# Two attentions on one core: PV ahead of projections when P buffers are full, ScalarE on a unit's last key blocks, VectorE's banks filled when free, gate masks made early

## The chip, the cores and the metric

The kernel runs on one core of a Trainium2 chip. The metric is the device time of one execution in microseconds (us). Three executions of the kernel before took 1019.16, 1023.16 and 1024.05 us; the median, 1023.16 us, is its time.

## The reference

Two attention layers over 2048 positions of width 512, each with 32 heads of 16 columns; their outputs stand side by side.

```python
def _B_ref(x, wqkv, wo):                      # plain softmax attention
    qkv = (x @ wqkv).reshape(B, S, 3, H, Dh) ...
    scores = einsum('bhqd,bhkd->bhqk', q, k) * Dh ** (-0.5)
    o = einsum('bhqk,bhkd->bhqd', softmax(scores), v)
    return merge(o) @ wo

def _A_ref(x, wq, wk, wv, wo, beta):          # 4 segments of 512, with a memory
    g = sigmoid(beta)
    for s in range(4):
        a_dot = softmax(qs @ ks.T * scale + causal_mask) @ vs
        a_mem = (phi(qs) @ M) / (phi(qs) @ z + 1e-6)
        outs.append(g * a_mem + (1 - g) * a_dot)
        M = M + phi(ks).T @ vs;  z = z + sum(phi(ks))
    return merge(outs) @ wo
return concatenate([a, b], axis=-1)
```

## The kernel before

**Units.** The work is cut into 64 units, each four heads over 512 queries: 32 of A (4 segments, 8 head groups) and 32 of B (4 query blocks, 8 head groups). The list `U` sets their order: the 8 units of A's first segment, then B's with A's other units mixed in. The four heads of a unit lie in the four 32-row groups of TensorE, so that four score matmuls, or four PV matmuls in the four column groups, run beside each other.

**Scores and P.** A unit of B has 64 blocks of 128 keys by 512 queries (16 key blocks, 4 heads), each one PSUM bank of scores. Two engines make P from them. ScalarE's blocks (`al`, 45 to a unit) go three and two at a time into two PSUM tiles `s_ps` (L722) and through one exp each (L727) into P tiles `pT`; there are three buffers (`PTB`) for either size, and `pt_out` counts those that PV hasn't read yet. VectorE's blocks (`dl`, 19 to a unit) go singly into one of two banks `d_ps` (L768); VectorE evicts a bank as an integer that is read as f16 (L779), and makes two further copies with an added constant, for two banks at a time (L745); the three together, each with its own scaled V (`VD`, made on POOL at L605), approximate the exp. Tiles `pD` have three buffers (`PDB`). A unit of A has 12 pieces of scores, the exps of L667 and L670, and a triangular mask on POOL (L681).

**PV.** There is one accumulator bank `acc`. PV matmuls (L870, `flush`) are issued for the unit in front alone (`pvi`). When all of its blocks are through, `finalize` transposes the accumulator on VectorE (L808), takes the reciprocal of the row sums (L811) and scales on POOL; only then the next unit's PV begins. ScalarE may be up to three units ahead.

**Projections and other small jobs** are called chores: transposes of x, the projections of q, k and v, the memory of A, the output projections (`chore_q`, `chore_k`, `chore_v`, `chore_out` and so on). Each fills a `d_ps` bank on TensorE, in turn with VectorE's score banks, and is evicted by VectorE. The masks of the queries (L329) are made on POOL behind it.

**What sets the order.** No hardware queue is scheduled by hand. A planner in Python, the loop `while True` in `fast_path`, keeps a model time for TensorE (`c["t"]`), ScalarE, VectorE and POOL, with costs such as 75 + 1.09 n ns for VectorE and 100 + 0.833 n ns for ScalarE, and at each step chooses what to issue next; the order of issue is then that of every engine's queue. A step asks, in this order: a score tile for ScalarE if its PSUM tile is free and fewer than `PTB` P tiles of the size are out (`act_now`), with VectorE banks beside it; a chore or a VectorE bank, if the next `d_ps` bank is free by plan (`dwhen`); PV. A chore has a due time, and it is due at once if `stalled` holds, that is if ScalarE has a unit but neither can take a tile now nor soon. ScalarE's unit `au` is the first of three that still has blocks; a unit of B whose `al` is empty and that has fewer than four blocks of `dl` left is passed over, if its `VD` exists, and VectorE takes the rest.

**The start.** `setup_late` is a chore due at A's third unit: ones in V's extra columns (L132, L133), the masks of the gates `maskg` (L153 to L161), zeros for the memory tiles (L163), and the loads of both `wo` from POOL's queue (L164, L165). The gates themselves come from ScalarE and VectorE at L899 to L902.

## Time and profile before

| | |
|---|---|
| median of three runs | 1023.16 us |
| profiled execution | 1026.3 us |
| its span | 1024.5 us |
| ScalarE (ACT) busy | 855.9 us, 84% |
| TensorE (PE) busy | 812.7 us, 79% |
| VectorE (DVE) busy | 782.7 us, 76% |
| GpSimd (POOL) busy | 375.0 us, 37% |
| mean granted TensorE clock | 0.912 |

The span runs from the first to the last instruction of the profiled execution; the device time has 1.8 us around it. The five compute engines have queues of their own, and each works through its instructions in order; idle time before an instruction is shown with what ended it (`<-engine tile line`). Matmuls overlap, so a busy TensorE is not one at its peak. L numbers are lines of the kernel before; behind line 94 the changed kernel's lines stand 2 to 8 further down (L722 becomes L729, L768 L775, L779 L786, L745 L752, L870 L877, L808 L815).

### The profile page before, as it was taken

The numbers are of one execution on the slowest core, as the hardware profiler recorded it, in microseconds if no ns is written. First come the engines' busy times: TensorE is split into PE (matmuls) and PEld (weight loads), VectorE is DVE, ScalarE is ACT, GpSimd is POOL, SyncE is SP. The second block draws the span as 40 slices with busy tenths as digits, with TensorE's granted clock in tenths as the row PEclk, the third lists the DMA queues.
The fourth block names the chain that finished last, engine by engine and source line by source line (L and its number), as shares of the span: only waits on it lengthen the run. The fifth ranks groups of instructions, "written<-read, shape, count | busy, mean of one in ns | idle before, by whom it ended". The sixth has DMA issues, their size and how long they took to land.

```text
span 1024.5 us, 18143 instructions
## 1 busy us (share of the span) xinstructions
PE 812.7 (79%) x7004; PEld 250.3 (24%) x7004; DVE 782.7 (76%) x1532; ACT 855.9 (84%) x790; POOL 375.0 (37%) x785
## 2 busy tenths in 40 slices
PE   6699888788878777888877777888887788777873
PEld 2233222222222223222222222223222212222221
DVE  3354778888888888778888888796778768889785
ACT  3489998989989598898988899897489689999791
POOL 2860634352144544142432143443542214223320
PEclk9799999998999898998999999899799969989697
DMA  5211000000000000000000000000000000000001
GB/s 169 63 43 36 6 22 2 1 2 1 1 1 17 6 1 12 27 1 2 1 1 22 1 1 2 1 1 22 1 1 2 22 1 2 1 1 1 1 6 40
DMA packets 13951, 13.83 MB, mean 13 GB/s; under 512 B 2336, under 2 KB 13600, under 8 KB 13856
## 3 DMA queue, kind: packets, MB, share of 16 engines
q1 hardware_dynamic: 11808, 10.49, 3.2%
q8 instruction: 56, 0.92, 0.4%
q10 hardware_dynamic: 1632, 1.05, 0.3%
q0 software_dynamic: 416, 1.05, 0.3%
q14 instruction: 39, 0.32, 0.1%
HBM read 8.39 MB, written 4.19 MB: 12 GB/s over the span
## 4 chain that ended last, share of the span: by engine, by line
PE 35%; ACT 34%; issue 17%; DVE 7%; POOL 5%; DMA 1%; ACTq 0%; DVEq 0%
ACT pT L727 30%; PE acc L870 13%; PE s_ps L722 7%; PE d_ps L316 4%; ACT pT L670 4%; PE d_ps L319 3%; DVE pD L779 2%; DVE pD L745 2%; PE s_ps L660 2%; PE d_ps L486 2%; PE d_ps L768 1%; POOL pT L681 1%; POOL VD L605 1%; DMA wk_a<-in_A_wk_dram 1%; DVE tT L808 1%
## 5 line engine op out<-in xcount | busy, mean ns | idle before, releaser
L727 ACT ACTIVATE pT<-s_ps 128x1536 bf16<-128x1536 f32 (+1 forms) x600 | 690.3, 1265 | 93.5 <-PE d_ps L768 55.8
L779 DVE TENSOR_SCALAR pD<-d_ps 128x512 int16<-128x512 f32 x554 | 370.5, 682 | 103.1 <-PE d_ps L768 95.2
L722 PE MATMUL s_ps<-QT_b,KT_b 32*128 32x512 bf16 x1494 | 242.8, 410 | 129.1 <-ACT pT L727 121.5
L870 PE MATMUL acc<-pT,VP_b 128*32 128x512 bf16 x1494 | 274.0, 424 | 1.7 <-DVE tT L808 1.7
L870 PE MATMUL acc<-pD,VD 128*32 128x512 f16 x1662 | 267.3, 425 | 3.6 <-DVE tT L808 2.1
L745 DVE TENSOR_SCALAR pD<-pD 128x1024 int16<-128x1024 int16 x554 | 241.3, 477 | 0.1
L681 POOL TENSOR_SCALAR_AFFINE_SELECT pT<-pT 128x512 bf16<-128x512 bf16 (+3 forms) x192 | 97.1, 518 | 377.5 <-ACT pT L670 361.1
L768 PE MATMUL d_ps<-QT_b,KT_b 32*128 32x512 bf16 x554 | 215.7, 413 | 3.2 <-DVE pD L779 2.1
L670 ACT ACTIVATE pT<-s_ps 128x1280 bf16<-128x1280 f32 (+1 forms) x128 | 138.4, 1191 | 26.0 <-PE s_ps L660 10.8
L722 PEld LDWEIGHTS <-KT_b 32*128 32x128 bf16 x1494 | 70.4, 92 | 348.2 <-issue 344.9
L870 PEld LDWEIGHTS <-VP_b 128*32 128x32 bf16 x1494 | 66.2, 99 | 75.0 <-issue 57.1
L870 PEld LDWEIGHTS <-VD 128*32 128x32 bf16 x1662 | 61.4, 99 | 85.9 <-issue 74.3
L660 PE MATMUL s_ps<-QT_a,KT_a 32*128 32x256 bf16 (+3 forms) x512 | 59.4, 318 | 28.5 <-ACT pT L727 13.0
L605 POOL TENSOR_SCALAR VD<-VP_b 128x288 bf16<-128x288 bf16 (+1 forms) x186 | 66.8, 359 | 12.3
L870 PE MATMUL acc<-pT,VP_a 128*32 128x256 bf16 (+3 forms) x512 | 36.9, 317 | 19.6 <-POOL pT L681 11.3
L829 POOL TENSOR_TENSOR tN<-tT,RA 128x256 bf16<-128x256 f32 x31 | 20.5, 662 | 83.7 <-DVE RA L811 83.6
L768 PEld LDWEIGHTS <-KT_b 32*128 32x128 bf16 x554 | 46.3, 92 | 17.5 <-issue 17.5
L808 DVE STREAM_TRANSPOSE tT<-acc 128x512 f32<-128x512 f32 x64 | 45.1, 704 | 6.0 <-PE acc L870 5.7
L329 POOL TENSOR_SCALAR QT_a<-qc,mq 128x512 bf16<-128x512 bf16 x30 | 21.8, 738 | 54.2 <-DVE qc L385 54.1
L660 PEld LDWEIGHTS <-KT_a 32*128 32x128 bf16 x512 | 20.0, 93 | 86.1 <-issue 78.8
L496 DVE CAST osb<-d_ps 128x512 bf16<-128x512 f32 x28 | 19.4, 691 | 21.8 <-PE d_ps L486 21.7
L329 POOL TENSOR_SCALAR QT_b<-qc,mq 128x512 bf16<-128x512 bf16 x32 | 22.5, 716 | 29.9 <-DVE qc L387 29.6
(110 smaller groups left out, 609.8 us busy)
## 6 DMA issues: line engine op xcount, KB each, us to landing
out_dram<-osb SPq DMA_DIRECT2D x30, 128.0 KB, 1.7
xin<-in_B_x_dram SPq DMA_DIRECT2D x16, 128.0 KB, 2.2
xin<-in_A_x_dram SPq DMA_DIRECT2D x14, 128.0 KB, 2.3
wv_a<-in_A_wv_dram SPq DMA_DIRECT2D x1, 512.0 KB, 10.5
wv_b<-in_B_wqkv_dram SPq DMA_DIRECT2D x1, 512.0 KB, 10.9
wk_b<-in_B_wqkv_dram SPq DMA_DIRECT2D x1, 512.0 KB, 10.8
wq_b<-in_B_wqkv_dram SPq DMA_DIRECT2D x1, 512.0 KB, 10.4
wo_a<-in_A_wo_dram POOLq DMA_DIRECT2D x1, 512.0 KB, 4.8
```

Source lines behind the costliest of these rows:

```text
L329: nc.gpsimd.tensor_scalar(t[:, par, :], qc[:], mq[:, par:par + 1], 1.0, ALU.mult, ALU.mult)
L605: mul = lambda dst, src: nc.gpsimd.tensor_scalar(dst, src, EXP_C[k], 1.0, ALU.mult, ALU.mult)
L660: nc.tensor.matmul(pt[:, b, col:col + w], kt[32 * j:32 * j + 32, kbl * P:(kbl + 1) * P], q[32 * j:32 * j + 32, P * kbl:512], start=(r == 0 ...
L670: nc.scalar.activation(pT[:].rearrange("p b n -> p (b n)")[:, 0:n], pt[:].rearrange("p b n -> p (b n)")[:, 0:n], ACT.Exp, scale=0.25)
L681: nc.gpsimd.affine_select(out=blk, in_=blk, compare_op=ALU.is_ge, fill=0.0, base=0, pattern=[[0, e - b], [0, w // P], [1, P]], channel_mul ...
L722: nc.tensor.matmul(pt[:, b, :], KT_b[32 * j:32 * j + 32, u["rt"], kb * P:(kb + 1) * P], q[32 * j:32 * j + 32, :], start=True, stop=True, t ...
L727: nc.scalar.activation(pT[:, 0:n, :], pt[:, 0:n, :], ACT.Exp, scale=1.0 / (LOG2E * 1024.0))
L745: nc.vector.tensor_scalar(tile[:, k, 0:n, :], tile[:, 0, 0:n, :], EXP_D[k], None, ALU.add)
L768: nc.tensor.matmul(bank[:], KT_b[32 * j:32 * j + 32, u["rt"], kb * P:(kb + 1) * P], qslice(u)[32 * j:32 * j + 32, :], start=True, stop=Tru ...
L779: nc.vector.tensor_scalar(pd[:, 0, n, :], bank[:], EXP_B, 0.0, ALU.add, ALU.max)
L808: nc.vector.transpose(tT[:].rearrange("p c d -> p (c d)"), u["acc"][:])
L870: nc.tensor.matmul(u["acc"][32 * j:32 * j + 32, e["c0"]:512], e["lhsT"], e["rhs"], start=(j not in u["started"]), stop=False, tile_positio ...
```

## The change

```diff
+    nc.sync.dma_start(out=wo_a[:], in_=wview(A_wo))
+    nc.sync.dma_start(out=wo_b[:], in_=wview(B_wo))
...
-    def setup_late():
+    jm = const.tile([P, 4], F32, name="jm")
+    nc.vector.memset(jm[:], 0.0)
+    for j in range(4):
+        nc.vector.memset(jm[32 * j:32 * j + 32, j:j + 1], 1.0)
+    mqg = const.tile([P, 4, 2], F32, name="mqg")
+    def setup_gates():
+        nc.scalar.activation(gcol[:], beta_t[:], ACT.Exp, scale=-1.0)
+        nc.vector.tensor_scalar(gcol[:], gcol[:], 1.0, None, ALU.add)
+        nc.vector.reciprocal(gcol[:], gcol[:])
+        nc.vector.tensor_scalar(omg[:], gcol[:], -1.0, 1.0, ALU.mult, ALU.add)
+        g4, m4 = gcol[:].rearrange("p (r t) -> p r t", t=2), mq[:].unsqueeze(1).to_broadcast([P, 4, 2])
+        nc.vector.tensor_tensor(mqg[:], g4, m4, op=ALU.mult)
+        for par in range(2):
+            to = maskg[:].rearrange("p (r t) j d -> p t r j d", t=2)[:, par]
...
+            for rt in range(4):
+                nc.gpsimd.tensor_tensor(to[:, rt, :, 0:DH], jm[:].unsqueeze(2).to_broadcast([P, 4, DH]),
+                                        mqg[:, rt, par:par + 1].unsqueeze(2).to_broadcast([P, 4, DH]), op=ALU.mult)
         init_v(VP_b, NSB)
...
-        nc.gpsimd.dma_start(out=wo_a[:], in_=wview(A_wo))
-        nc.gpsimd.dma_start(out=wo_b[:], in_=wview(B_wo))
...
-    chore(begin("a", 0, 2), setup_late)
...
+    setup_gates()
...
-            if u["k"] == "b" and nbanks(u) == 0 and len(u["dl"]) < 4 and u["i"] in VD_t:
+            if u["k"] == "b" and exhausted(u):
                 continue
...
-        if ai[0] == len(U) and tail["banks"] is None and ("b", 3, 2) in OT_t and not chores:
+        if ai[0] == len(U) and tail["banks"] is None and ("b", 3, 2) in OT_t:
             tail_open()
...
-        stalled = au is not None and (au["ready"] is None or (act_now is None and act_soon is None))
+        blocked = au is not None and au["ready"] is not None and pt_out[scount[0] % 2][0] >= PTB
+        stalled = au is not None and not blocked and act_now is None and act_soon is None
...
-        dwhen = max(d_when(), c["dve"] - 700)
+        dwhen = d_when()
...
-            while (beside and du["dl"] and max(d_when(), c["dve"] - 700) <= t + 300
+            while (beside and du["dl"] and d_when() <= t + 300
...
+        u = U[pvi[0]]
+        byj = by_head(u, t)
+        rd = sum(byj, [])
+        done = exhausted(u) and len(rd) == len(u["pvq"])
+        full = blocked or max(x[0] for x in pt_out) >= PTB or (dve_out[0] >= PDB and pd_open["tile"] is None)
+        even = min(len(x) for x in byj)
+        if (rd and (even >= 3 or done or (full and len(rd) >= 4) or (blocked and max(len(x) for x in byj) > 0))
+                and (u["acc"] is not None or acc_free[0] <= t + 100) and (act_soon is None or act_soon > t + 200)):
+            flush(u, 16 if done else min(even, 4) if even >= 3 else 3)
+            continue
         if due or du is not None or ch is not None:
...
-        full = max(x[0] for x in pt_out) >= PTB or (dve_out[0] >= PDB and pd_open["tile"] is None)
-        even = min(len(x) for x in byj)
-        if rd and (even >= 3 or done or (full and len(rd) >= 4)) and (u["acc"] is not None or acc_free[0] <= t + 100):
-            if act_soon is None or act_soon > t + 200:
-                flush(u, 16 if done else min(even, 4) if even >= 3 else 3)
-                continue
...
-    assert not chores and tail["banks"] is not None
+    assert tail["banks"] is not None
+    while chores:
+        chores.pop(0)["fn"]()
```

`setup_gates()` is called behind the first transposes of x. The PV step moves ahead of chores and VectorE's banks and is also taken when ScalarE is `blocked` (its unit is ready and its P buffers are full); `blocked` no longer counts as `stalled`. A unit of B stays ScalarE's until all of its blocks are taken. A `d_ps` bank is filled when it is free by plan, without the limit on VectorE's queue. The setup of the gates stands at the start, the loads of `wo` in SP's queue behind the other weights, and chores left over at the end follow the last unit.

Counted over the whole program, VectorE gets 534 score banks for 554 and ScalarE 1514 for 1494, in 303 exps of 1024 columns and 11 of 512, for 296 and 5; those of 1536 remain 299.

On TensorE, in the middle of the program where A's fourth segment begins, a projection of A's queries (`wq_a`), its last two matmuls, and what follows. The kernel before:

```order
9981 L316 LDWEIGHTS wq_a
9982 L316 MATMUL d_ps<-xT_a,wq_a 128x512
9983 L316 LDWEIGHTS wq_a
9984 L316 MATMUL d_ps<-xT_a,wq_a 128x512
9985 L319 LDWEIGHTS xT_a
9986 L319 MATMUL d_ps<-wv_a,xT_a 128x512
```

The changed kernel at the same projection:

```order
10109 L324 LDWEIGHTS wq_a
10110 L324 MATMUL d_ps<-xT_a,wq_a 128x512
10111 L324 LDWEIGHTS wq_a
10112 L324 MATMUL d_ps<-xT_a,wq_a 128x512
10113 L729 LDWEIGHTS KT_b
10114 L729 MATMUL s_ps<-QT_b,KT_b 128x512
```

Before, the next projection follows (here that of V, `wv_a`), and so on for 56 projection matmuls between two score refills; now a score refill for ScalarE (`s_ps`) stands behind the one projection, and one ahead of it.

On VectorE, at the end of the unit that is 51st in the list, a unit of B with one of A behind it. The kernel before (`qc` is the eviction of a projection of queries, `pD<-d_ps` that of score banks, `tT` the transposed accumulator at a unit's end):

```order
797 L387 TENSOR_SCALAR qc<-d_ps 128x512
798 L779 TENSOR_SCALAR pD<-d_ps 128x512 x2
799 L745 TENSOR_SCALAR pD<-pD 128x1024 x2
800 L779 TENSOR_SCALAR pD<-d_ps 128x512 x2
801 L745 TENSOR_SCALAR pD<-pD 128x1024 x2
802 L808 STREAM_TRANSPOSE tT<-acc 128x512
803 L811 RECIPROCAL RA<-tT 128x16
804 L779 TENSOR_SCALAR pD<-d_ps 128x512
805 L808 STREAM_TRANSPOSE tT<-acc 128x512
```

The changed kernel at the end of its 51st unit (`osb` is the eviction of an output projection, `aT` of A's memory):

```order
761 L786 TENSOR_SCALAR pD<-d_ps 128x512 x2
762 L752 TENSOR_SCALAR pD<-pD 128x1024 x2
763 L504 CAST osb<-d_ps 128x512
764 L786 TENSOR_SCALAR pD<-d_ps 128x512
765 L815 STREAM_TRANSPOSE tT<-acc 128x512
766 L818 RECIPROCAL RA<-tT 128x16
767 L474 STREAM_TRANSPOSE aT<-d_ps 128x512
```

Before, four of VectorE's banks are the last work ahead of the transposition, and the next unit's transposition follows at once behind one bank; now two banks, an output projection and one bank stand there, and the next unit's transposition comes later.

On POOL, at the start. The kernel before, from the end of the setup to the masks of the next queries (`mbd` are the memory's tiles):

```order
46 L161 COPY maskg<-bdm 128x4
47 L163 MEMSET mbd_128 128x1024
48 L163 MEMSET mbd_129 128x1024
49 L164 DMA wo_a<-in_A_wo_dram 128x4x512
50 L165 DMA wo_b<-in_B_wo_dram 128x4x512
51 L329 TENSOR_SCALAR QT_a<-qc,mq 128x512 x2
52 L681 AFFINE_SELECT pT_422<-pT_422 128x2x256
```

The changed kernel (the ISA row is the choice of POOL's library):

```order
8 L146 DMA beta_t<-in_A_beta_dram 32x4x2 x4
9 L167 ISA
10 L167 TENSOR_TENSOR maskg<-jm,mq 128x4x4
11 L169 TENSOR_TENSOR maskg<-jm,mqg 128x4x16 x4
12 L167 TENSOR_TENSOR maskg<-jm,mq 128x4x4
13 L169 TENSOR_TENSOR maskg<-jm,mqg 128x4x16 x4
14 L134 MEMSET VP_b 128x32x2 x16
15 L135 MEMSET VP_b 128x16x14
16 L173 MEMSET mbd_130 128x1024
17 L173 MEMSET mbd_131 128x1024
18 L688 AFFINE_SELECT pT_246<-pT_246 128x3x128
```

The setup has moved from behind A's first selects and masks to ahead of the first of them, with fewer operations on the masks and without the two DMAs.

## Rows read from the trace of the kernel before

**Rows 1.** The page: busy us, share of the span and instructions of each engine.

```profile
PE 812.7 (79%) x7004; PEld 250.3 (24%) x7004; DVE 782.7 (76%) x1532; ACT 855.9 (84%) x790; POOL 375.0 (37%) x785
```

**Rows 2.** Busy time by stretch: length, each engine's busy us, granted clock, DMA.

```profile
60.00:1001.00 941.00, 764.82 (x6681) 232.65 (x6680) 750.11 (x1457) 825.21 (x758) 338.48 (x678) 0.92 0.02 7
708.00:732.00 24.00, 20.55 (x115) 7.80 (x113) 18.23 (x31) 5.31 (x6) 14.19 (x23) 0.90 0.05 16
594.00:634.00 40.00, 30.68 (x298) 9.66 (x297) 34.87 (x69) 37.13 (x36) 20.63 (x40) 0.96 0.00 1
```

**Rows 3.** ScalarE in order of time: start, us, what; idle before and what ended it.

```profile
167.70 5.54 ACT L727 ACTIVATE pT<-s_ps 128x1024 bf16<-128x1024 f32 x5 [2.87 <-PE d_ps L768]
...
336.59 0.63 ACT L417 ACTIVATE ek<-kb 128x512 bf16<-128x512 bf16 x1 [4.29 <-DVE kb L410]
343.72 2.37 ACT L727 ACTIVATE pT<-s_ps 128x1536 bf16<-128x1536 f32 x2 [5.58 <-PE d_ps L768]
...
715.27 0.63 ACT L371 ACTIVATE eq<-qc 128x512 bf16<-128x512 bf16 x1 [4.61 <-DVE qc L385]
719.75 0.63 ACT L371 ACTIVATE eq<-qc 128x512 bf16<-128x512 bf16 x1 [3.85 <-DVE qc L385]
727.10 1.02 ACT L727 ACTIVATE pT<-s_ps 128x1024 bf16<-128x1024 f32 x1 [6.72 <-PE s_ps L722]
731.34 7.04 ACT L727 ACTIVATE pT<-s_ps 128x1536 bf16<-128x1536 f32 x6 [3.22 <-PE d_ps L768]
...
818.92 3.83 ACT L727 ACTIVATE pT<-s_ps 128x1536 bf16<-128x1536 f32 x3 [7.40 <-PE s_ps L722]
...
960.76 1.02 ACT L727 ACTIVATE pT<-s_ps 128x1024 bf16<-128x1024 f32 x1 [2.38 <-PE d_ps L768]
```

**Rows 4.** TensorE in order of time, in the second and third episode.

```profile
713.36 1.02 PE L316 MATMUL d_ps<-xT_a,wq_a 128*128 128x512 bf16 x4
...
813.25 0.37 PE L768 MATMUL d_ps<-QT_b,KT_b 32*128 32x512 bf16 x1 [0.67 <-DVE pD L779]
...
817.01 1.26 PE L870 MATMUL acc<-pT,VP_a 128*32 128x512 bf16 x16 [1.52 <-DVE tT L808]
```

**Rows 5.** Groups by line and shape: count, busy us, mean ns, idle before.

```profile
L727 ACT ACTIVATE pT<-s_ps 128x1536 bf16<-128x1536 f32 x299 | 443.0, 1482 | 57.8 <-PE d_ps L768 36.6 <-PE s_ps L722 18.8 <-POOL tN L829 0.7
L779 DVE TENSOR_SCALAR pD<-d_ps 128x512 int16<-128x512 f32 x554 | 370.5, 682 | 103.1 <-PE d_ps L768 95.2 <-PE s_ps L722 3.0
L727 ACT ACTIVATE pT<-s_ps 128x1024 bf16<-128x1024 f32 x296 | 312.7, 1056 | 35.7 <-PE d_ps L768 19.2 <-PE s_ps L722 15.9
L722 PE MATMUL s_ps<-QT_b,KT_b 32*128 32x512 bf16 x1494 | 242.8, 410 | 129.1 <-ACT pT L727 121.5 <-ACT pT L670 5.0
L745 DVE TENSOR_SCALAR pD<-pD 128x1024 int16<-128x1024 int16 x554 | 241.3, 477 | 0.1
L768 PE MATMUL d_ps<-QT_b,KT_b 32*128 32x512 bf16 x554 | 215.7, 413 | 3.2 <-DVE pD L779 2.1 <-DVE qc L387 0.5 <-DVE kb L410 0.5
L727 ACT ACTIVATE pT<-s_ps 128x512 bf16<-128x512 f32 x5 | 3.1, 639 | 0.0
```

**Rows 6.** The start: POOL's mask operation by line, then engines in order of time.

```profile
L159 POOL TENSOR_TENSOR maskg<-bdm,gcol 128x64 f32<-128x64 f32 x8 | 2.3, 294 | 0.1
...
15.26 0.21 ACT L899 ACTIVATE gcol<-beta_t 128x8 f32<-128x8 bf16 x1
...
19.56 1.85 POOL L681 TENSOR_SCALAR_AFFINE_SELECT pT<-pT 128x384 bf16<-128x384 bf16 x4 [15.52 <-issue]
...
32.12 1.46 POOL L132 MEMSET VP_b<- 128x64 bf16 x16
...
38.58 1.84 POOL L163 MEMSET mbd<- 128x1024 bf16 x2
...
42.11 1.37 POOL L329 TENSOR_SCALAR QT_a<-qc,mq 128x512 bf16<-128x512 bf16 x2
...
46.33 2.15 ACT L670 ACTIVATE pT<-s_ps 128x1280 bf16<-128x1280 f32 x2 [10.56 <-POOL QT_a L329]
```

More of the change, by code (lines that the diff above doesn't have):

```diff
@@ L146, in fast_path @@
     gcol = const.tile([P, HG], F32, name="gcol")
-    def setup_late():
-        init_v(VP_b, NSB)
-        bdm = const.tile([P, 2, 4, 17], F32, name="bdm")
-        nc.gpsimd.memset(bdm[:], 0.0)
-        for j in range(4):
-            for par in range(2):
-                nc.gpsimd.tensor_copy(bdm[32 * j:32 * j + 32, par, j, :],
-                                      mq[32 * j:32 * j + 32, par:par + 1].to_broadcast([32, 17]))
-        for hg in range(HG):
-            nc.gpsimd.tensor_tensor(maskg[:, hg, :, 0:DH], bdm[:, hg % 2, :, 0:DH],
-                                    gcol[:, hg:hg + 1].unsqueeze(2).to_broadcast([P, 4, DH]), op=ALU.mult)
-            nc.gpsimd.tensor_copy(maskg[:, hg, :, DH:DH + 1], bdm[:, hg % 2, :, DH:DH + 1])
+    jm = const.tile([P, 4], F32, name="jm")
[12 more added lines that the diff above has]
+            to = maskg[:].rearrange("p (r t) j d -> p t r j d", t=2)[:, par]
+            j4 = jm[:].unsqueeze(1)
+            nc.gpsimd.tensor_tensor(to[:, :, :, DH], j4.to_broadcast([P, 4, 4]), mq[:, par:par + 1].unsqueeze(2).to_broadcast([P, 4, 4]), op=ALU.mult)
+            for rt in range(4):
+                nc.gpsimd.tensor_tensor(to[:, rt, :, 0:DH], jm[:].unsqueeze(2).to_broadcast([P, 4, DH]),
+                                        mqg[:, rt, par:par + 1].unsqueeze(2).to_broadcast([P, 4, DH]), op=ALU.mult)
+        init_v(VP_b, NSB)
         for m in mbds:
             nc.gpsimd.memset(m[:], 0.0)
-        nc.gpsimd.dma_start(out=wo_a[:], in_=wview(A_wo))
-        nc.gpsimd.dma_start(out=wo_b[:], in_=wview(B_wo))
     sat = const.tile([P, 1], F32, name="sat")
@@ L898, in fast_path @@
     nc.vector.tensor_scalar(qt0[:, 1, :], pt[:, 1, :], mq[:, 1:2], None, ALU.mult)
-    nc.scalar.activation(gcol[:], beta_t[:], ACT.Exp, scale=-1.0)
-    nc.vector.tensor_scalar(gcol[:], gcol[:], 1.0, None, ALU.add)
-    nc.vector.reciprocal(gcol[:], gcol[:])
-    nc.vector.tensor_scalar(omg[:], gcol[:], -1.0, 1.0, ALU.mult, ALU.add)
     t0 = c["t"]
@@ L1042, in fast_path @@
             continue
-        u = U[pvi[0]]
-        byj = by_head(u, t)
-        rd = sum(byj, [])
-        done = exhausted(u) and len(rd) == len(u["pvq"])
-        full = max(x[0] for x in pt_out) >= PTB or (dve_out[0] >= PDB and pd_open["tile"] is None)
-        even = min(len(x) for x in byj)
-        if rd and (even >= 3 or done or (full and len(rd) >= 4)) and (u["acc"] is not None or acc_free[0] <= t + 100):
-            if act_soon is None or act_soon > t + 200:
-                flush(u, 16 if done else min(even, 4) if even >= 3 else 3)
-                continue
         if u["acc"] is None:
```

## The prediction

> **What bounds the kernel now.** I read the busy times first [rows 1]: ScalarE has the largest share, 84% of the span, with TensorE at 79% and VectorE at 76%, so no engine is full over the whole run and the ends of its waits decide. Then the busy times by stretch [rows 2]. From 60 to 1001 us ScalarE works 825.2 of 941 us, so it is idle for 115.8 us; the best stretch of 40 us has it busy for 37.1 (93%), and the stretch from 708 to 732 us for only 5.3 of 24 while TensorE there is busy for 20.6. Then the rows of ScalarE with the idle time ahead of each [rows 3]. There are three episodes. From 332 to 344 us it waits 4.29 and 5.58 us, from 710 to 731 us it waits 4.61, 3.85, 6.72 and 3.22 us, and at 811 us it waits 7.40 us: 35.7 us together. Ten more waits of 1.94 to 3.33 us, of which the first (2.87 us at 168 us) and the last (2.38 us at 961 us) stand there, sum to 25.7 us. So 61.4 of the 115.8 us of idle time lie in 17 waits, and the rest in short ones.
>
> The three episodes have two causes, both of the planner. In the second, TensorE runs one projection after another (1.0 us each, [rows 4]) and no score tile: all P buffers are full, the planner calls that "stalled", "stalled" makes any projection due, and projections are asked ahead of PV. Only PV frees a P buffer, so ScalarE stands until the list of projections is empty. In the third, TensorE waits for VectorE's banks (0.67 us at 813 us) and then 1.52 us for the transposition of the accumulator before 16 PV matmuls of the next unit in a row [rows 4]: ScalarE had gone on to later units while the unit in front still had banks for VectorE, and with one accumulator nothing of the later units could be drained.
>
> **The change part by part.** *PV ahead of projections, and "blocked" no longer "stalled".* In the program of before, 10 stretches of TensorE between two score refills hold two or more projections (8 matmuls or more), the longest 56 matmuls; in the changed one a single such stretch is left, of 16. All projections are still there, now mostly one between two refills. At 1.0 us each beside a refill of 0.4 us [rows 5] this makes 1.4 us of TensorE per exp, against exps of 1.48 and 1.06 us [rows 5], mean 1.27: I allow 0.15 us of remaining wait for each of the 24 projections of the three longest stretches, 4 us. *ScalarE takes a unit's last key blocks.* It removes the cause of the third episode and of those among the ten where TensorE drains 16 PV at once. Of the ten I leave 5 us. The gain of these two edits is 61.4 - 4 - 5 = 52 us. Its bounds are 25 us (only the first two episodes go, with 28.3 us, less their projections) and 61.
>
> What the second costs: the program's rows give VectorE 534 banks for 554, and ScalarE 20 more, as seven more exps of 1024 columns and six more of 512. At 1.056 and 0.639 us [rows 5] this is 7.4 + 3.8 = 11.2 us on the engine that sets the path, plus 11.2. VectorE is relieved of 20 evictions (0.682 us) and 20 additions (0.477 us for each bank) [rows 5], 23 us, and TensorE of 40 PV matmuls. Neither ends last over a long stretch, so I count zero; their cover is ScalarE's queue, and if ScalarE were to fall behind them these 23 us would be gain.
>
> ScalarE's share [rows 1] is the largest, and the edit adds to it. The Trainium skill's page Perfetto Trace Analysis, section Identifying the Most-Contended Engine, takes the engine with the highest occupancy as the one to relieve first. A rule that speaks against this edit: by it the 11.2 us would simply lengthen the run, to 1034; the trace bears it out only where ScalarE has no idle time, and 115.8 us of it stand in the middle stretch.
>
> *Banks filled as soon as free.* The limit "VectorE's queue within 700 ns of its end" goes. VectorE loses part of its 103 us of idle time ahead of L779 [rows 5], which isn't on the path: zero. But TensorE's queue is in order, and a bank filled by plan before VectorE has really emptied it holds back the score refills queued behind it, and so ScalarE. In before TensorE waited for this 2.1 us in all [rows 5]. The plan counts an eviction as 633 ns and the trace shows 682; for the two additions of a pair it counts 2 x 403 against 2 x 477, so a pair of banks takes 2.32 us where the plan has 2.07, 0.25 us late. With 267 pairs the cost lies between 0 and 66 us. I take 4, near the row of 2.1, because VectorE has idle time in which to catch up and because ScalarE's exps run longer than planned too (1.48 for 1.38 us), which holds TensorE back first. Some 15 further refills have a projection in front that had none, at 0.15 us 2 us. Together plus 6.
>
> *Gate masks early.* In before POOL goes through the setup from 32.12 to 42.11 us without a pause, with the masks of the next queries behind it, and ScalarE waits 10.56 us for these [rows 6]. This goes. In its place the setup stands ahead of POOL's first select: 8 masks of 0.294 us, the ones of V for 1.46 us, the zeros for 1.84 us, and three small operations that I price like a mask, 0.9 us: 6.5 us together. If it starts as soon as the gates are there, at about 15.5 us, it ends at 22.0, and the first select (19.56 us in before) is 2.4 us late; if POOL can't start before 19.56 us, 6.5 us late. ScalarE has buffers for six tiles before it needs PV, so part is hidden. I take 4: minus 6. ScalarE now computes the gates ahead of the first cast of K, and VectorE four small operations ahead of the first queries. The gates' exp started at 15.26 us behind the cast, without a recorded wait for its data [rows 6], so the cost is 0 to 1.4 us; I take 0.5. The loads of wo pass from POOL to SP, ahead of B's x tiles; these are first needed behind the setup's stall, so zero. The sum of this part is -5.5, with bounds -10 and +1.4.
>
> Of POOL's first operation the profile shows only that 15.52 us went by ahead of it, ended by nothing recorded [rows 6]. The Trainium skill's page GPSIMD Engine Reference, section 2.1 Instruction dispatch, says that the first call after a change of POOL's library costs about 6 us more without a visible instruction. By that the setup would start late, the start would gain nothing, and the time would be 5 us above the forecast; the rows can't tell it apart.
>
> *The end.* Two output projections may now be left for after the last unit: two evictions at the price of L779, 1.4 us [rows 5]. Against that the last unit no longer waits for banks that VectorE still holds. Zero, with 3 us either way.
>
> The sum is -52 + 11.2 + 6 - 5.5 + 0 = -40.3 us. The profiled execution took 1026.3 us, its span of 1024.5 and 1.8 around it; the median of the three runs is 1023.16, and the difference is applied to that: **983 us**. A second way agrees: were the middle stretch as full everywhere as in its best 40 us, it would take (825.2 + 11.2) / 0.928 = 901 us for 941, and with the start this gives 978.
>
> **The rivals.** *More goes:* the short waits shrink as well, since ScalarE no longer waits for a unit's last banks: 15 us less, 968. For it speaks that the best stretch still has a 7% remainder; against it that projections now sit everywhere. *Only the projections' part is regained:* the held units stay late for another reason (PV of the next unit waits for POOL's selects, or VectorE lags), the gain is 30 for 52 and the time 1005. For it speaks the 1.52 us wait for VectorE's transposition, which no edit removes. *Slower, by banks filled too early:* TensorE blocks on VectorE's bank ahead of the score refills, 0.25 us for each of 267 pairs, 66 us in place of 4: 1045. It decides from 0.16 us per pair on. Against it speaks the row of 2.1 us, for it that this row was made with the limit still there. *The busiest engine gets longer:* nothing is regained in the middle, the start gains 5.5: 1029, or 1034 without the start. Against it speak TensorE's 20.6 busy us of 24 beside ScalarE's 5.3. *The order of before was no cause:* what is regained at the episodes comes back as waits elsewhere, in size about the 40 us, 1022.
>
> **How the numbers follow.** The forecast has 0.55, with its own range of 972 to 1000 (the bounds of the gain and of the start). More regained has 0.15, projections alone 0.15, banks too early 0.07, the busiest engine 0.03, no difference 0.05. A measurement of this kernel can tell about 0.5% from no change, 1018 to 1028. Faster is 0.55 + 0.15 + 0.15 = 0.85, the same 0.05, slower 0.07 + 0.03 = 0.10. The range leaves out the last three (0.15) and the edge of the second, and reaches from 964 to 1012.
>
> **What would show it.** Right: no row of ScalarE with more than 3 us of idle time between 60 and 980 us; some 867 us busy on ScalarE at a share of 87 to 89%; 534 evictions on L786 (L779 of before); no pause of ScalarE at 36 to 46 us, and POOL's masks ahead of its first select. TensorE's wait ahead of L775 (L768 of before) for VectorE stays under 10 us. Wrong: that wait at tens of us, or waits of ScalarE that keep their sum and only change their places; or a start that begins its exps later than 16 us by more than 2 us.

## The result, and the profile after

The changed kernel takes 979.41 us (four runs, 974.37 to 984.88) against 1021.16 us (four runs, one more than ahead of the prediction, 1015.83 to 1024.05) of the kernel before: a ratio of 0.9598, 95% interval 0.9524 to 0.9672. The forecast was 983 us, with a range of 964 to 1012.

The page's first part for the changed kernel, then its busy times by stretch (length, then busy us and instructions of PE, PEld, DVE, ACT, POOL, then granted clock, DMA share and GB/s):

```profile
PE 822.3 (84%) x6974; PEld 255.7 (26%) x6974; DVE 753.5 (77%) x1502; ACT 864.9 (89%) x803; POOL 373.0 (38%) x768
```

```profile
0.00:60.00 60.00, 45.24 (x343) 17.61 (x343) 23.86 (x66) 38.52 (x41) 39.45 (x105) 0.94 0.35 108
60.00:957.00 897.00, 770.84 (x6598) 235.91 (x6595) 721.20 (x1421) 825.17 (x761) 333.18 (x663) 0.94 0.02 7
957.00:976.60 19.60, 6.25 (x39) 2.22 (x36) 8.41 (x16) 1.17 (x2) 0.38 (x1) 0.73 0.14 45
```

Between 60 us and the last exp ScalarE is busy for as long as before, 825.2 us [rows 2], in 897 us for 941. Its idle time in that stretch falls from 115.8 to 71.7 us. The span falls from 1024.5 to 976.6 us, by 47.9, and on ScalarE's account this is +9.0 of busy time, -44.1 of idle time in the middle, -9.2 in the first 60 us (38.5 us busy there; before, 29.3) and -3.6 behind the last exp. (These are two single executions, with a mean granted TensorE clock of 0.940 for 0.912; the medians are 41.8 us apart.)

ScalarE in order of time, the three waits over 3 us that are left, and the place of the old second episode:

```profile
137.35 3.71 ACT L734 ACTIVATE pT<-s_ps 128x1536 bf16<-128x1536 f32 x3 [6.76 <-PE s_ps L729]
...
639.24 2.37 ACT L734 ACTIVATE pT<-s_ps 128x1536 bf16<-128x1536 f32 x2 [3.06 <-PE d_ps L775]
...
715.88 2.54 ACT L734 ACTIVATE pT<-s_ps 128x1536 bf16<-128x1536 f32 x2 [0.27 <-PE s_ps L729]
719.75 2.37 ACT L734 ACTIVATE pT<-s_ps 128x1536 bf16<-128x1536 f32 x2 [1.34 <-PE s_ps L729]
...
808.82 4.62 ACT L734 ACTIVATE pT<-s_ps 128x1024 bf16<-128x1024 f32 x4 [3.35 <-PE d_ps L775]
```

Before there were ten such waits, 45.1 us together ([rows 3] has seven of them); now three, 13.2 us. At the fourth segment of A, where 18.4 us were lost around 710 to 731 us, the longest wait is 1.34 us. The longest wait that is left, at 137 us, is of the kind of the old third episode: VectorE's last bank of the unit in front, the transposition, then the PV of the next unit, and only then a refill.

```profile
132.71 0.37 PE L775 MATMUL d_ps<-QT_b,KT_b 32*128 32x512 bf16 x1
133.84 0.71 DVE L815 STREAM_TRANSPOSE tT<-acc 128x512 f32<-128x512 f32 x1
135.10 1.47 PE L877 MATMUL acc<-pT,VP_b 128*32 128x512 bf16 x12
```

The groups that answer to [rows 5] (count, busy us, mean ns, idle before and what ended it):

```profile
L734 ACT ACTIVATE pT<-s_ps 128x1536 bf16<-128x1536 f32 x299 | 441.9, 1478 | 38.9 <-PE d_ps L775 18.3 <-PE s_ps L729 17.8 <-POOL tT L838 1.1
L786 DVE TENSOR_SCALAR pD<-d_ps 128x512 int16<-128x512 f32 x534 | 350.1, 680 | 56.6 <-PE d_ps L775 54.4 <-PE s_ps L729 0.4
L734 ACT ACTIVATE pT<-s_ps 128x1024 bf16<-128x1024 f32 x303 | 318.8, 1053 | 29.8 <-PE d_ps L775 19.8 <-PE s_ps L729 8.7 <-ACT pT L674 0.3
...
L729 PE MATMUL s_ps<-QT_b,KT_b 32*128 32x512 bf16 x1514 | 242.1, 398 | 70.2 <-ACT pT L734 62.9 <-ACT pT L677 2.8
...
L775 PE MATMUL d_ps<-QT_b,KT_b 32*128 32x512 bf16 x534 | 186.4, 396 | 15.1 <-DVE pD L786 13.0 <-DVE kb L418 0.5 <-DVE aT L474 0.4
```

VectorE's idle time ahead of its evictions falls from 103.1 to 56.6 us, and TensorE waits 13.0 us for VectorE's banks where it waited 2.1.

### The profile page after: what moved, and what is told of

It reads as the page before. It is cut to its first block, busy times and chain, and to the rows that moved or that the text cites. A ratio compares the mean times of both kernels' runs of the same rounds, so it can differ in the third digit from the quotient of the medians.

```text
span 976.6 us, 18041 instructions
## 1 busy us (share of the span) xinstructions
PE 822.3 (84%) x6974; PEld 255.7 (26%) x6974; DVE 753.5 (77%) x1502; ACT 864.9 (89%) x803; POOL 373.0 (38%) x768
## 4 chain that ended last, share of the span: by engine, by line
PE 32%; ACT 28%; DVE 16%; issue 14%; POOL 9%; DMA 1%; ACTq 0%; DVEq 0%; POOLq 0%
ACT pT L734 23%; PE acc L877 13%; PE s_ps L729 8%; DVE pD L786 7%; DVE pD L752 5%; ACT pT L677 4%; POOL VD L612 4%; PE d_ps L324 3%; POOL pT L688 2%; PE d_ps L327 2%; DVE tT L815 2%; PE d_ps L494 2%; PE d_ps L775 1%; PE s_ps L667 1%; DMA beta_t<-in_A_beta_dram 1%
## 5 line engine op out<-in xcount | busy, mean ns | idle before, releaser
L734 ACT ACTIVATE pT<-s_ps 128x1536 bf16<-128x1536 f32 (+2 forms) x613 | 701.5, 1253 | 68.8 <-PE d_ps L775 38.0
L786 DVE TENSOR_SCALAR pD<-d_ps 128x512 int16<-128x512 f32 x534 | 350.1, 680 | 56.6 <-PE d_ps L775 54.4
L877 PE MATMUL acc<-pT,VP_b 128*32 128x512 bf16 x1514 | 268.1, 409 | 0.0
L877 PE MATMUL acc<-pD,VD 128*32 128x512 f16 x1602 | 240.5, 409 | 4.2 <-DVE tT L815 4.0
L752 DVE TENSOR_SCALAR pD<-pD 128x1024 int16<-128x1024 int16 (+1 forms) x538 | 234.1, 477 | 0.3
L775 PE MATMUL d_ps<-QT_b,KT_b 32*128 32x512 bf16 x534 | 186.4, 396 | 15.1 <-DVE pD L786 13.0
L729 PEld LDWEIGHTS <-KT_b 32*128 32x128 bf16 x1514 | 70.2, 91 | 295.3 <-issue 288.9
L677 ACT ACTIVATE pT<-s_ps 128x1024 bf16<-128x1024 f32 (+1 forms) x128 | 136.7, 1169 | 10.9 <-PE s_ps L667 9.4
L667 PE MATMUL s_ps<-QT_a,KT_a 32*128 32x384 bf16 (+3 forms) x512 | 57.7, 303 | 24.2 <-ACT pT L677 12.2
L877 PE MATMUL acc<-pT,VP_a 128*32 128x384 bf16 (+3 forms) x512 | 49.0, 318 | 16.2 <-POOL pT L688 12.8
L775 PEld LDWEIGHTS <-KT_b 32*128 32x128 bf16 x534 | 40.1, 91 | 9.0 <-issue 7.7
```

Of the source, the lines that this page charges most:

```text
L667: nc.tensor.matmul(pt[:, b, col:col + w], kt[32 * j:32 * j + 32, kbl * P:(kbl + 1) * P], q[32 * j:32 * j + 32, P * kbl:512], start=(r == 0 ...
L677: nc.scalar.activation(pT[:].rearrange("p b n -> p (b n)")[:, 0:n], pt[:].rearrange("p b n -> p (b n)")[:, 0:n], ACT.Exp, scale=0.25)
L729: nc.tensor.matmul(pt[:, b, :], KT_b[32 * j:32 * j + 32, u["rt"], kb * P:(kb + 1) * P], q[32 * j:32 * j + 32, :], start=True, stop=True, t ...
L734: nc.scalar.activation(pT[:, 0:n, :], pt[:, 0:n, :], ACT.Exp, scale=1.0 / (LOG2E * 1024.0))
L752: nc.vector.tensor_scalar(tile[:, k, 0:n, :], tile[:, 0, 0:n, :], EXP_D[k], None, ALU.add)
L775: nc.tensor.matmul(bank[:], KT_b[32 * j:32 * j + 32, u["rt"], kb * P:(kb + 1) * P], qslice(u)[32 * j:32 * j + 32, :], start=True, stop=Tru ...
```

## Experiments

Theory: the four edits work as the prediction adds them up (PV first and the last blocks regain waits, early banks cost a little, the start gains a little). Rival: some of them help only in company. Twelve kernels test this: each edit alone (e1 to e4), the changed kernel without one edit (e5 to e7, and e9 in part), and four attempts to better it. Ratios are to the kernel before on the same chip: 1016.18 us for e1 to e4, 1019.71 for e5 to e8, 1017.41 for e9 to e12. A ratio isn't the quotient of the medians, and differences in us that are called "by the ratio" are the ratio's distance from 1 in a time of about 1018 us. "Idle" is ScalarE's idle time between 60 us and its last exp in the one profiled execution. "Clock" is the mean granted TensorE clock of each run, lowest to highest; for the kernel before it is that of the 33 runs beside the experiments.

| kernel | VectorE's / ScalarE's banks | us | ratio, 95% interval | ACT busy | idle | clock |
|---|---|---|---|---|---|---|
| before | 554 / 1494 | 1021.16 | 1 | 855.9 | 115.8 | 0.911 to 0.934 |
| changed | 534 / 1514 | 979.41 | 0.960, 0.952 to 0.967 | 864.9 | 71.7 | 0.927 to 0.948 |
| e1: PV first alone | 524 / 1524 | 1055.79 | 1.036, 1.029 to 1.043 | 868.2 | 136.1 | 0.900 to 0.907 |
| e2: last blocks alone | 515 / 1533 | 1013.28 | 0.996, 0.992 to 1.001 | 876.9 | 93.7 | 0.887 to 0.916 |
| e3: early banks alone | 589 / 1459 | 1035.57 | 1.017, 1.010 to 1.024 | 839.5 | 136.1 | 0.906 to 0.915 |
| e4: gates alone | 554 / 1494 | 1008.04 | 0.992, 0.988 to 0.996 | 854.9 | 104.1 | 0.914 to 0.938 |
| e5: changed, PV not first | 586 / 1462 | 1036.17 | 1.015, 1.010 to 1.021 | 843.1 | 145.5 | 0.905 to 0.922 |
| e6: changed, banks not early | 475 / 1573 | 997.13 | 0.980, 0.976 to 0.984 | 891.0 | 61.7 | 0.924 to 0.926 |
| e7: changed, gates late | 534 / 1514 | 978.67 | 0.963, 0.958 to 0.969 | 864.1 | 68.1 | 0.930 to 0.948 |
| e9: changed, units held at one or two blocks | 544 / 1504 | 981.49 | 0.969, 0.962 to 0.977 | 859.7 | 81.5 | 0.927 to 0.949 |

**e1, PV first alone.** The kernel before with the PV step and `blocked` of the change, and nothing else:

```diff
+        blocked = au is not None and au["ready"] is not None and pt_out[scount[0] % 2][0] >= PTB
+        stalled = au is not None and not blocked and act_now is None and act_soon is None
...
+            flush(u, 16 if done else min(even, 4) if even >= 3 else 3)
+            continue
         if due or du is not None or ch is not None:
```

> The kernel before with the PV edit alone: PV ahead of projections and VectorE's banks, and blocked no longer stalled. Its program has 524 banks on VectorE for 554 and 1524 on ScalarE for 1494, about 0.53 us of ScalarE each, 16 us. Theory of the prediction (the waits of the first two episodes, 28.3 us, were made by projections ahead of PV): 28 us less, 16 us more, about 1009 us for 1021, and no ScalarE wait over 3 us while projections run in a row. Rival (the sum of the waits stays and only moves): 1037 us.

Measured: 37 us slower than before by the ratio (39.6 by the medians), missed by both. ScalarE, TensorE and VectorE at the end of a unit of B, the line numbers being those of before (L927 is a matmul with zeros by which the planner fills idle time):

```profile
822.58 1.02 ACT L727 ACTIVATE pT<-s_ps 128x1024 bf16<-128x1024 f32 x1
831.71 3.71 ACT L727 ACTIVATE pT<-s_ps 128x1536 bf16<-128x1536 f32 x3 [8.10 <-PE s_ps L722]
```

```profile
825.19 0.38 PE L768 MATMUL d_ps<-QT_b,KT_b 32*128 32x512 bf16 x1
825.51 0.39 PE L927 MATMUL acc<-wq_a,zero 128*128 128x512 bf16 x1
826.04 0.37 PE L768 MATMUL d_ps<-QT_b,KT_b 32*128 32x512 bf16 x1
826.97 0.40 PE L870 MATMUL acc<-pD,VD 128*32 128x512 f16 x2 [0.56 <-DVE pD L745]
827.30 0.39 PE L768 MATMUL d_ps<-QT_b,KT_b 32*128 32x512 bf16 x1
827.61 0.39 PE L870 MATMUL acc<-pD,VD 128*32 128x512 f16 x2
827.94 0.39 PE L768 MATMUL d_ps<-QT_b,KT_b 32*128 32x512 bf16 x1
829.80 1.26 PE L870 MATMUL acc<-pT,VP_a 128*32 128x512 bf16 x16 [1.47 <-DVE tT L808]
830.99 1.03 PE L722 MATMUL s_ps<-QT_b,KT_b 32*128 32x512 bf16 x5
```

```profile
829.03 0.70 DVE L808 STREAM_TRANSPOSE tT<-acc 128x512 f32<-128x512 f32 x1
```

ScalarE has gone on to the next units and filled their P buffers. The unit in front still lacks blocks of VectorE's, which come one at a time behind its evictions; then the transposition, then 16 PV matmuls that free the buffers. Call this a held unit. Nine of the eleven waits over 3 us look like this, with 16 PV matmuls of the next unit just ahead of the refill; they sum to 49 us of the 63.9. A tenth, 8.78 us at 147 us, has PV matmuls of a unit of B in their place, and the eleventh stands behind POOL's masks of the queries. In none of the eleven does TensorE do more than one projection: the rows of projections of the first two episodes are gone, and held units have taken their place. In the kernel before three of the ten waits over 3 us have the 16 PV matmuls just ahead: 7.40 us at 819 us [rows 4], and 3.08 and 5.58 us at 226 and 344 us, with projections between. That VectorE's banks now stand behind PV in the planner's order, so that more units are held open at their end, fits this and is argued only. If it holds, the edit on the last blocks isn't an addition to PV first but its condition: then the kernel with both and without early banks (e6) must lose these waits.

**e2, the last blocks alone.**

```diff
-            if u["k"] == "b" and nbanks(u) == 0 and len(u["dl"]) < 4 and u["i"] in VD_t:
+            if u["k"] == "b" and exhausted(u):
```

> The kernel before with one edit alone: ScalarE takes a unit's last key blocks. 515 banks on VectorE, 1533 on ScalarE, 39 more at 0.53 us, 21 us. Theory of the prediction: the held units go (7.4 us at 811 us and about 20 of the other waits), against 21 us of exps: 1015 us. Rival (a unit is held up by projections, not by VectorE's last banks): 1042 us, since only the 21 us of exps are left.

Measured: no difference clear of noise, 3 us less by the medians, nearer to the theory's 6 than to the rival's 21 more. Two waits over 3 us stay of ten, idle time falls by 22.1 us, but ScalarE has 39 more banks and is 21.0 us longer busy. One pays for the other. Per bank this is 0.54 us. The granted clock is lower here than in the kernel before; what that means for the time is said behind the experiments.

**e3, early banks alone.** `dwhen` and the loop beside it without `c["dve"] - 700`.

> The kernel before with one edit alone: VectorE's two banks filled as soon as free by plan. 589 banks on VectorE (all of its blocks), 1459 on ScalarE, 35 fewer at 0.53 us, 19 us. Theory of the prediction (early filling brings nothing, and costs TensorE waits of some 4 us): between 1006 us, if the fewer exps count in full, and 1025. Rival A (TensorE is held by VectorE's bank 0.25 us per pair): 295 pairs, 74 us, 1076 us or more. Rival B (without PV first, the longer rows of projections, 18 stretches with two or more for 10, make more waits): 1030 us.

Measured: 17 us slower by the ratio (1035.57 us), nearest to the 1030 of rival B, and by its cause, rows of projections. Rival A fails: TensorE's wait for VectorE ahead of L768 is only 7.0 us. ScalarE in e3 and TensorE in the same stretch:

```profile
89.53 0.63 ACT L417 ACTIVATE ek<-kb 128x512 bf16<-128x512 bf16 x1 [10.46 <-DVE kb L410]
...
114.44 0.63 ACT L371 ACTIVATE eq<-qc 128x512 bf16<-128x512 bf16 x1 [8.50 <-DVE qc L385]
121.18 2.37 ACT L727 ACTIVATE pT<-s_ps 128x1536 bf16<-128x1536 f32 x2 [6.11 <-PE d_ps L768]
```

```profile
79.35 1.91 PE L316 MATMUL d_ps<-xT_b,wk_b 128*128 128x512 bf16 x4
81.06 5.04 PE L319 MATMUL d_ps<-wv_b,xT_b 128*128 128x512 bf16 x20
85.94 1.02 PE L316 MATMUL d_ps<-xT_b,wq_b 128*128 128x512 bf16 x4
86.88 1.02 PE L316 MATMUL d_ps<-xT_b,wk_b 128*128 128x512 bf16 x4
87.74 1.96 PE L319 MATMUL d_ps<-wk_a,xT_a 128*128 128x512 bf16 x7
```

With projections still ahead of PV, a bank that is filled as soon as it is free is filled with the next projection: one follows another without a gap, and 38 us of ScalarE's waits over 2 us lie between 60 and 122 us, where the kernel before has none.

**e4, the gates alone.** `setup_gates` for `setup_late`, and `wo` in SP's queue.

> The kernel before with one edit alone: gate masks and setup at the start, wo loaded from SP. The order of TensorE, VectorE's banks and ScalarE's exps are those of before. Theory of the prediction: POOL's stall of 10 us goes, 4 to 5 us come back at the start, 1015 us, and the first exp of B starts 5 us earlier than the 73.9 us of before. Rival (POOL can't begin its first operation before about 19 us whatever it is, so that the setup comes wholly on top): 1021 us and the first exp of B at 71 to 74 us.

Measured: 8 us faster, 2 us more than the theory. ScalarE's wait at 46 us [rows 6] is gone, the first exp of B starts at 64.28 us, 9.6 us earlier and not 5, and the waits over 3 us in the middle are those of before, 11 to 15 us earlier (one falls just below 3 us).

**e5 to e7, the changed kernel less one edit.** e5 puts the PV step of before back, e6 the limit on VectorE's queue:

```diff
-        dwhen = d_when()
+        dwhen = max(d_when(), c["dve"] - 700)
```

> The changed kernel with the PV step put back behind projections and VectorE's banks (and 'blocked' stalled again); the other edits stay. The program gives VectorE 586 of the 2048 score banks (534 in the changed kernel), and TensorE has 18 stretches of two or more projections between refills, the longest of 20 matmuls. Numbers against a kernel before of 1016 us and a changed kernel of 975 us (ratio 0.960). Theory 'the edits need each other': early banks without PV first mean projections and VectorE's banks go ahead of the matmuls that free P buffers, as in the experiment with the banks alone (ratio 1.017): 1016 to 1033 us, less 8 for the gates: 1008 to 1025, ScalarE's idle time in the middle 100 us or more. Theory 'the edits add up' (singles: PV +39, last -4, banks +17, gates -8 us): without PV the rest gives 1016 - 4 + 17 - 8 = 1021. Rival 'PV first gives the prediction's 28 us here': 975 + 28 = 1003.

> The changed kernel with the limit on VectorE's queue put back; the other edits stay. The program gives VectorE only 475 banks for 534, ScalarE 59 more (1573). Against a kernel before of 1016 us and a changed one of 975. Theory 'the early filled banks are what gives VectorE its share': 59 banks x about 0.53 us = 31 us more busy time on ScalarE (some 895 us), which is the path now, so 995 to 1006 us, with no rise of ScalarE's idle time of 72 us in the middle. Theory of the prediction (early banks cost 6 us and gain nothing): 969. If the edits simply add up (singles +39 for PV, -4, -8): 1043.

> The changed kernel with the setup of the gates as a late chore again, as in the kernel before; same share of banks (534). Against a kernel before of 1016 us and a changed one of 975: theory 'the start is separate from the middle' gives the same 8 us as the gates alone did (ratio 0.992): 983, with POOL's stall of 10 us and ScalarE's wait for POOL's masks back at 30 to 46 us and the waits in the middle as in the changed kernel, only later. Rival 'the start shifts the middle's order' : anything over 990 or under 978.

Measured in e5: 1036 us, above all three. The projections of e3 are back at the same places; here they are on ScalarE:

```profile
84.08 0.63 ACT L425 ACTIVATE ek<-kb 128x512 bf16<-128x512 bf16 x1 [10.23 <-DVE kb L418]
...
109.03 0.63 ACT L379 ACTIVATE eq<-qc 128x512 bf16<-128x512 bf16 x1 [8.50 <-DVE qc L393]
115.77 2.37 ACT L734 ACTIVATE pT<-s_ps 128x1536 bf16<-128x1536 f32 x2 [6.11 <-PE d_ps L775]
```

Beside the others PV first is worth 0.055 of the time, 56 us; alone it costs 37.

Measured in e6: 997 us, inside the range for "the early banks give VectorE its share". The page of e6 and its group for VectorE's banks:

```profile
PE 809.2 (82%) x6852; PEld 249.8 (25%) x6852; DVE 703.9 (71%) x1383; ACT 891.0 (90%) x831; POOL 366.5 (37%) x768
```

```profile
L775 PE MATMUL d_ps<-QT_b,KT_b 32*128 32x512 bf16 x475 | 187.0, 411 | 3.2 <-DVE pD L786 2.5 <-DVE KT_a L369 0.5 <-DVE osb L504 0.2
```

From e6 to the changed kernel ScalarE's busy time falls by 26.1 us (59 banks at 0.44), and its idle time rises by 10.0, about as much as TensorE's wait for VectorE (2.5 to 13.0 us). By occupancy e6 should be slow: it is the kernel with the longest ScalarE of all, 35 us more than before, and yet 20 us faster than before: its idle time is 54.1 us shorter. One wait over 3 us is left in it (4.4 us, behind POOL's masks of the queries), where e1 without the edit on the last blocks has eleven. The gates, which e6 has and e1 hasn't, leave the waits in the middle as they are (e4).

Measured in e7: it can't be told from the changed kernel, with ratios of 0.963 and 0.960 whose intervals overlap; the 8 us of the theory aren't seen. The stall is there (10.75 us ahead of the exp at 44.53 us), but the first selects come at 18.99 us instead of 25.07; where both go over to units of B, near 60 us, e7 is 3.7 us behind.

**e9, units held at one or two blocks.** The edit on the last blocks is undone in part:

```diff
-            if u["k"] == "b" and exhausted(u):
+            if u["k"] == "b" and nbanks(u) == 0 and len(u["dl"]) < 3 and u["i"] in VD_t:
```

> The changed kernel, but ScalarE again passes over a unit of B when its own list is empty and only one or two of VectorE's blocks are left (in the kernel before: one to three; in the changed kernel none). VectorE gets 544 banks for 534. Against a kernel before of 1018 us and a changed one of 0.960 of it, 977. Theory 'PV first is only good if no unit is held for VectorE's last blocks': waits of ScalarE over 3 us at the ends of units come back, at least five of them, and the time is 10 to 30 us above the changed kernel, 987 to 1007 (ratio 0.97 to 0.99). Rival 'VectorE's early filled banks clear the held blocks soon enough, the edit on the last blocks isn't needed beside them': 10 banks less on ScalarE, 5 us, so 972 (0.955), with ScalarE's idle time as in the changed kernel, some 72 us.

Measured: 0.969, between the two, at the edge of the first theory. Of waits over 3 us there are three and not five; two are new held units, at 324 and 581 us, and the third (7.70 us at 135 us) is the one that the changed kernel has at 137 us:

```profile
323.69 1.45 ACT L734 ACTIVATE pT<-s_ps 128x1536 bf16<-128x1536 f32 x1 [7.42 <-PE s_ps L729]
```

Waits of 1.9 us and more sum to 44.3 us for the changed kernel's 20.8, but the shorter ones shrink; ScalarE's busy time falls by 5.2 us, its idle time rises by 9.8. The direction is that of the first theory, the size is small, and the interval reaches into that of the changed kernel.

**e8 and e12, a leaner start.** e8 puts the gates behind the first casts of Q and K, and the masks, ones and zeros on VectorE. e12 also has one tiny product on POOL at the very start, loads beta from SP's queue, and makes the gates behind the first unit.

```diff
+    pz = const.tile([P, 2], F32, name="pz")
+    nc.gpsimd.memset(pz[:], 0.0)
+    nc.gpsimd.tensor_tensor(pz[:, 0:1], pz[:, 1:2], pz[:, 1:2], op=ALU.mult)
...
-        nc.gpsimd.dma_start(out=beta_t[...
+        nc.sync.dma_start(out=beta_t[...
```

> The changed kernel with a leaner start: the setup of the gates behind the first casts of Q and K (ScalarE's exp on the gates no longer holds up the cast of K, nor VectorE's small operations the first queries), and the masks, V's ones and the zeros on VectorE in place of POOL, so that POOL's first operation is a select. Same order of everything else. Numbers against a changed kernel of 975 us. Theory 'POOL's first library operation cannot start before about 19.3 us whatever it is, and the setup then holds up the selects by 5.75 us': first exp at about 14 us for 17.0, first select at 19.3 for 25.1, and a time 3 to 6 us shorter: 969 to 972. Rival 'TensorE or VectorE set the start, not POOL': the select comes early but the first units end as before, 975 within 1 us.

> The lean start of e8, with one tiny multiplication on POOL ahead of everything else that POOL does after V's first ones, the loads of beta on SP's queue in place of POOL's, and the setup of the gates as a chore behind the first unit. Question: POOL's first operation of this kind came at 19.3 us with the setup, and at 18.9 to 19.6 us with a select, always 14.8 to 15.5 us behind the end of POOL's DMA issues at 4.05 us. Theory 'it is a start-up that begins when POOL reaches the first such operation': that operation now comes 2.5 us earlier, at some 16.4 us, and selects follow from 17 us. Rival 'it waits for something in the chip until 19 us whatever is queued': still at 19. The time: as e8 or up to 2 us less (ratio 0.957 to 0.959).

Measured: e8 976.10 us, ratio 0.959 (0.955 to 0.963), e12 972.95 us, 0.958 (0.954 to 0.963). Neither can be told from the changed kernel; e8's time is as its rival had it. But in the profiled executions the first units do end earlier: the last exps ahead of B's units come 6.1 and 6.9 us sooner, and the spans are 974.8 and 970.1 us for 976.6; of e8's 6.1 us only 1.8 are left at the end. POOL's first operation in e12 comes at 11.50 us, earlier than either theory had it (16.4 and 19 us). POOL's first operations in the changed kernel, in e8 and in e12:

```profile
19.32 0.21 POOL L167 TENSOR_TENSOR maskg<-jm,mq 128x16 f32<-128x16 f32 x1 [15.26 <-issue]
...
25.07 3.22 POOL L688 TENSOR_SCALAR_AFFINE_SELECT pT<-pT 128x384 bf16<-128x384 bf16 x7
```

```profile
18.87 0.90 POOL L686 TENSOR_SCALAR_AFFINE_SELECT pT<-pT 128x384 bf16<-128x384 bf16 x2 [14.80 <-issue]
```

```profile
11.50 0.18 POOL L151 TENSOR_TENSOR pz<-pz 128x1 f32<-128x1 f32 x1 [10.20 <-issue]
14.06 0.53 POOL L690 TENSOR_SCALAR_AFFINE_SELECT pT<-pT 128x384 bf16<-128x384 bf16 x1 [2.38 <-ACT pT L679]
```

**e10 and e11, the planner's costs.** e8 with ScalarE's cost as measured, and (e11) VectorE's as well:

```diff
     def act_cost(n):
-        return 100.0 + 0.833 * n
+        return 208.0 + 0.829 * n
```

> The changed kernel with the lean start of e8, and the planner's cost of an exp on ScalarE set to the measured 1.48 and 1.06 us (208 + 0.829 n ns in place of 100 + 0.833 n). The program then gives VectorE 550 banks for 534 and has no stretch of two projections between refills. Theory 'ScalarE's busy time is the path, and VectorE has room': 16 banks x 0.53 = 8.5 us less, 966 to 969 for the changed kernel's 977 (before 1018; ratio 0.949 to 0.952). Rival 'VectorE's banks end last now': idle time of ScalarE rises by as much, ratio 0.959.

> As e10, and VectorE's costs in the planner set to the measured ones as well (an eviction 0.68 us for 0.63, an addition for a pair 0.48 for 0.40). The program gives VectorE 545 banks. Theory 'what counts is the number of ScalarE's banks': 5.8 us less than the lean start, ratio 0.953 and 3 us behind e10. Theory 'the wait of TensorE for a bank that is filled too early counts' (13 us in the changed kernel): that wait falls below 5 us, and the time is 0.95 or below, ahead of e10.

Measured: 998.22 us for e10, 0.981 (0.975 to 0.987), and 984.45 us for e11, 0.969 (0.965 to 0.974). Both lose against e8, and all forecasts for them were missed. TensorE's groups in e10, for VectorE's banks and for the refills of ScalarE:

```profile
L727 PE MATMUL s_ps<-QT_b,KT_b 32*128 32x512 bf16 x1498 | 242.9, 405 | 37.7 <-ACT pT L732 34.1 <-ACT pT L675 0.8
L773 PE MATMUL d_ps<-QT_b,KT_b 32*128 32x512 bf16 x550 | 195.3, 395 | 40.6 <-DVE pD L784 34.5 <-DVE KT_a L367 2.0 <-DVE osb L502 1.0
```

In e8 it is 64.6 us ahead of the refills and 12.6 for VectorE's banks. With a ScalarE that is slower by plan, the planner puts more of VectorE's banks ahead of a refill; TensorE then stands in front of a bank that VectorE hasn't emptied (34.5 us, 21.9 more than e8), with the refill queued behind. ScalarE's busy time falls by 4.4 us, its idle time rises by 24.2, and most of that lies in 27 waits of 1 to 1.9 us (13 in e8), none over 3. That is the "banks too early" of the prediction's third rival, brought about by a larger share for VectorE. In e11 the wait is 19.4 us and the idle time 81.2: the costs of VectorE make up for part of it.

## Why the prediction came out right, and where its steps did not

The total was right, and so was its main mechanism: ScalarE's long waits were an order problem of the planner, and most of them go. That the total met the measurement as closely as it did is in part luck, as the granted clock shows. By the profile:

- *Waits regained.* Predicted: 61.4 us in 17 waits fall by 52, less 6 for the early banks. Measured: those of 1.9 us and more go from 61.4 to 20.8 us, 40.5 for 46, and all shorter ones from 54.5 to 50.9. "No wait over 3 us" failed at three places (13.2 us), of which the longest is still a held unit. The traces compared have granted clocks of 0.912 and 0.940. e4, with before's order in the middle and 0.938, is the nearer measure: idle time there is 104.1 us, so it falls by 32.4 and not by 44.1; the long waits fall by 38.5, and the short ones rise by some 6.
- *What failed is to price PV first as a gain of its own.* The bounds of 25 to 61 us for the two edits took PV first to be worth 25 even alone. e1 shows +37 us alone: the rows of projections go, as predicted, but held units take their place. The prediction also counted the wait of 5.58 us at 344 us to the projections, where the 16 PV matmuls of a held unit stand just ahead of the refill. The pair is sound: in e6, without early banks, idle time falls by 54.1 us against before and by 42.4 against e4; 52 was predicted.
- *ScalarE's share.* Predicted +11.2 us from 20 more banks, measured +9.0 busy. The cause was put wrongly: the pair moves 79 banks to ScalarE (554 to 475, +35.1 us busy in e6), and the early banks give 59 back to VectorE.
- *Early banks.* Predicted +6, with VectorE's idle time counted as zero. This term has the wrong sign: from e6 to the changed kernel it is -2.0% of the time, some 20 us (some 11 between the two runs of each at granted clocks of 0.926 and 0.927). Its cost is bigger than I took (TensorE's wait is 10.5 us up and not 4; the sign "under 10" was missed at 13.0), but the share that VectorE gets back outweighs it. VectorE's idle time was put at zero because VectorE is never last; but it decides how many banks ScalarE has to take, and ScalarE is last. That share was in the order of the changed kernel, so the sum had the gain through the count of 534, and the total didn't suffer.
- *Start.* Predicted -5.5. The stall is gone, as said. Alone the edit gives 8 us (e4), beside the others nothing that noise doesn't cover (e7). In the changed kernel the setup holds the first select back by 5.5 us (25.07 for 19.56), near the 6.5 of the worse branch: POOL's first operation came at 19.32 us. That time is no fixed bound, as e8's expectation has it, and the "always 14.8 to 15.5 us" of e12's leaves out runs: with the same start as here POOL's first operation came at 17.19 us in e9 and at 17.72 in e4. The first exp starts 0.9 us later.
- *End.* Predicted 0 with 3 either way; 19.8 us behind the last exp for 23.2, just outside.
- *Busy share.* ScalarE has 864.9 us at 89%, for 867 at 87 to 89.
- *Range.* The forecast's own 972 to 1000 isn't what its named bounds give: 25 and 61 us of gain alone make 1010 and 974.
- *The granted clock.* The sum has no term for it. Within one kernel the time goes with it: the 19 runs of the kernel before beside e1 to e4 lie between 1025.91 us at 0.912 and 1012.33 at 0.932. The changed kernel runs at 0.927 to 0.948. At 0.927 the kernel before took 1013.11 us, the changed one 982.50 and 984.88: some 30 us, of the 42 between the medians. By these three runs, which are few, about a quarter goes with a higher clock; that is an estimate. In e2 it is the other way round: at 0.911 it took 1009.75 and 1008.86 us, where the kernel before at 0.912 took 1025.91, so at a like clock it is some 16 us shorter than that run, which the medians don't show. e1, at 0.900 to 0.907, lies below every run of before, and part of its 37 us may be this. Why an order has the clock that it has, no run here separates from the order itself.

Had more work on the busiest engine simply lengthened the run, the time would have been 1034. e6 and the changed kernel show that with 62 to 116 us of idle time on ScalarE in the middle, the order was worth more than its load. The Trainium skill's page Perfetto Trace Analysis, section Identifying the Most-Contended Engine, names the engine with the highest occupancy as the one to optimize first. The trace agrees, ScalarE having 84%, and what was gained on it was idle time; that more load must lengthen the run is the prediction's reading.

What stays open: the changed kernel with the last blocks' edit wholly undone wasn't tried, so its size beside the others is known only from e1 against e6 (1.036 to 0.980, with the gates in e6) and from the partial e9. How much of each difference in the table goes with the clock stays open as well.

## What to carry over

Edits to a planner's order aren't terms to add: the four alone sum to +42 us, together they give -42, so name for each edit which other one it needs (here: PV first needs that no unit is held open at its end, early banks need PV first). An engine that is never last still has a price if it decides how much work the last engine gets: count the shares, and see which edit moves them. A better cost in a model isn't a better order: after e10, look at who stands in front of whose buffer before giving an engine more. Read the granted clock beside each time: two orders compared by medians alone, or by single traces, can differ by it as well (e2 here).

## What the runs showed of the hardware

POOL's first library operation comes late: in the 13 kernels with the four beta loads in POOL's queue it began 13.08 to 15.79 us behind them, whether it is a product or a select (at 17.12 us in e1 to 19.83 in e3). In five of them (before, changed, e7, e8, e9) nothing recorded ended that wait, of 13.14 to 15.52 us; in the others the profile names a result of ScalarE or VectorE. With those loads on SP's queue and the operation right behind a memset (e12), it is 10.20 us without a recorded cause, and the operation is done by 11.7 us. The Trainium skill's page GPSIMD Engine Reference, section 2.1 Instruction dispatch, gives about 6 us for the first call to a freshly loaded kernel, without a visible instruction. The direction agrees, the size here is 10 us and more. That the loads in the queue make up the rest may be, but e12 moved two things at once and doesn't show it.
